# Four edits to a fused attention, MoE and soft-MoE kernel: zero products at the start, the remainder products moved, one copy moved to ScalarE, one weight load moved

## The chip, the core and the metric

The kernel runs on one core of a Trainium2 chip. The metric is the device time of one execution in microseconds, as the median of the executions timed.

## The reference, cut to what matters

Everything is float32. There are 4 batches, 12 heads, a sequence of S = 448 and a head size of 64.

```
scores = (q @ k.T) / 8 - log(448)
attn   = sigmoid(scores)              # no softmax: each score by itself
x      = (attn @ v), heads joined     # 1792 tokens x 768
x      = ((x @ w_a) * (x @ w_b)) @ w_out
logits = x @ phi                      # 32 columns
d      = softmax of logits over all 1792 tokens
c      = softmax of logits over the 32 columns
out    = c @ experts(d.T @ x)         # 8 experts, 4 slots each, two matrices w1, w2 with a relu between
```

## The kernel before

The heads are worked through in pairs: one step g of the attention is two heads, 6 steps to a batch, 24 in all (`NP` = 6, `GT0` = 13, `GQ` = 14). Of a step, `emit_TK` brings k and q into transposed form and splits each into a high and a low part (`split_heads`: a cast to fp32r and a subtraction), `emit_S` makes the scores of one chunk of keys as three products per head and hands each head's score tile to ScalarE (`sigmoid`, L249), and `emit_PV` multiplies with v. From step 13 on VectorE does the transposing (L191), before that TensorE (L195). From step 14 on a head's 448 keys are three chunks of 128 and a remainder of 64. The remainders of an even step and of the odd one after it share two tiles: `emit_S_rest` (L258) makes them, at the odd step's end, from `whole` (the q tile in place, and a copy of k's last 64 columns, `kr`, that ScalarE makes). `emit_PV` of the odd step ends with the products on them (L286).

`att()` is a generator that emits these pieces in a fixed order and yields after each. Nothing reorders them later: each engine runs its instructions in the order in which the program emits them. Around each piece the main loop (L1192) emits one step of whatever else is due: `fill_step` (the logits of a finished batch, `LG`, `logits`, `tokens`), `operands` (sums and splits of x for the products of batches 1 and 2, which go by a Strassen-like scheme in `unit`) and `prep_u` (the weights of the first unit, loaded by `load_u`).

PSUM has eight banks, shared out by tag: `ms` 2, `sc` 4, `ab` 2. `ms()` gives out the `ms` tag (later in the kernel, by a counter, also `sc`). A new tile of a tag takes a bank whose earlier tile has had its last reader, and the first instruction that writes it waits for that reader. Before the change the first chunk of step 13 (one head of two) and of the odd steps from 15 on is in `ms`, that of the even steps in `sc`; the remainders are in `ms`; `emit_PV` of steps 12 and 13 is in `ms`, from 14 on in `ab`; the logits of batch 0 are in `ab`, and the tile into which `tokens` transposes them (L935) is in `ms`. VectorE reads that tile out (L936).

The stages in time: batch 0's attention to 54 us, its two MoE products with batch 1's attention to 205, the attention of batches 2 and 3 to 280, the products of batches 1 and 2 (`unit`, L855) to 440, those of batch 3 (L667) to 544, and then the experts, whose weights come through a ring of SBUF slots that earlier stages leave free.

All loads of q, k and v are issued by SP in program order (`load_qkv`). The load for step g + 3 is emitted in `emit_TK` of step g, but for the q of steps 19 and 23, which `emit_S_rest` of steps 15 and 19 emits.

Of the kernel before, what the change touches and what calls it, by code (L numbers as in the profile page):

```python
# [41 lines left out]
def body(ctx, tc, q, k, v, w_a, w_b, w_out, phi, w1, w2, out):  # L42
# [68 lines left out]

    def consts():
        make_identity(nc, ident)
        dve.memset(nlog, -math.log(S))
        dve.memset(tiny, 2.0 ** -120)
        act.activation(rs, nlog, AF.Sigmoid)
        dve.tensor_tensor(e32, idj[:, 0], idj[:, 1], op=ALU.add)
        dve.tensor_tensor(e32, e32, idj[:, 2], op=ALU.add)
        dve.tensor_tensor(e32, e32, idj[:, 3], op=ALU.add)
        for j in range(1, 4):  # L120
            dve.tensor_copy(selF[:, j], e32)
# [8 lines left out]
    def load_qkv(g, names):  # L130
# [6 lines left out]
        for src, nm, n in ((k, "k", 3), (q, "q", 3), (v, "v", 3)):  # L137
# [31 lines left out]
            if nm == "v":  # L169
                t = t[:T].rearrange("p (h c d) -> p h c d", h=2, c=C)  # L170
                sp.dma_start(out=t, in_=s)
            else:
                t = t[:T].rearrange("p (c h d) -> p c h d", c=C, h=2)
                for h in range(2):
                    (sp if g or not h else act).dma_start(out=t[:, :, h], in_=s[:, h])
# [11 lines left out]
    def transposed(g, nm):  # L187
        a = qkv_t.pop((nm, g))
        if g >= GT0:
            a = a.rearrange("p n d -> p (n d)")  # L190
            dve.transpose(a, a)  # L191
            return a
        t = ms()
        for c in range(C):
            pe.transpose(t[:, c * T:(c + 1) * T], a[:, c].rearrange("p h d -> p (h d)"), ident[:T, :T])  # L195
        load_qkv(g + 3, nm)
        run["trans"] = True
        return t

    def emit_TK(g):  # L200
        if g >= B * NP:
            return
        if g >= GT0:
            for nm in "kq":
                t = transposed(g, nm)
                split_heads(g, nm, t, dve.tensor_copy)
                if g >= GQ:
                    if nm == "k":
                        kr = atp.tile([128, 64], F32, tag="kr", name="kr", bufs=3)
# [7 lines left out]
        if not g:  # L217
            tq = transposed(g, "q")
# [11 lines left out]
    def emit_S(g, chunks):  # L230
# [3 lines left out]
        for c in chunks:  # L234
            ab = (g < NP or 2 * NP < g < GQ) and c == 2
            by_ms = c == 0 and (g % 2 if g >= GQ else g >= GT0)
# [15 lines left out]
    def emit_S_rest(g):  # L252

        sc = [ms() for _ in range(2)]
# [65 lines left out]
    def att():  # L320
# [3 lines left out]
        for g in range(B * NP + 1):  # L324
# [8 lines left out]
            for c in first:  # L333
                emit_S(g, (c,))
                run["done"] = True
                yield 800
            if g:
# [22 lines left out]
            else:  # L360
# [7 lines left out]
                if g >= GQ and g % 2:  # L368
                    emit_S_rest(g)
                    yield 800  # L370
# [396 lines left out]
    def operands():  # L767
# [7 lines left out]
        for i in range(3):  # L775
            while 2 * NP + 3 + i not in xt:
                yield
# [107 lines left out]
    def logits(b):  # L885
# [11 lines left out]
        dve.tensor_reduce(mx, lf, axis=AX.X, op=ALU.max)  # L897
# [15 lines left out]
        if not b:  # L913
            dve.tensor_copy(ls, lf)
# [274 lines left out]
    then = [(GQ + 1, lambda: load_u(0)), (GQ + 5, lambda: reload_gk(0, 1, gk_01[1])),  # L1189
            (GQ + 6, lambda: load_u(1)), (GQ + 7, lambda: reload_gk(0, 0, gk_01[0])),  # L1190
            (GQ + 7, lambda: reload_gk(0, 2, gk_2))]
    for cost in att_g:  # L1192
# [5 lines left out]
        if next(ops, 0) == 0:  # L1198
# [226 lines left out]
```

## Time and profile before

| | us |
|---|---|
| median of 3 runs | 659.08 (658.64 to 660.87) |
| the profiled execution, its own time | 657.77 |
| span of the profiled execution, first to last instruction | 656.0 |

The profile is of one execution. Busy time of an engine is the sum over its instructions. PE is TensorE's products, PEld its weight loads, DVE is VectorE, ACT ScalarE, POOL GpSimd, SP the engine that issues most DMAs. A row of the timeline gives start and length in us, then engine, line, operation, and what is written from what; "x4" joins four such instructions, and brackets at the end give the engine's idle time before it and what ended that. A product in float32 stands as two instructions, one in fp32r as one.

### The profile page before, as it was taken

The page shows a single profiled execution, that of the slowest core. Times are in us where ns is not written, and L with a number is a line of the kernel's source. Part 1 is how long each engine was busy: PE and PEld are TensorE (multiplying, and loading weights), DVE is VectorE, ACT ScalarE, POOL GpSimd, SP SyncE. Part 2 cuts the span into 40 slices and gives each one's busy share as a digit, 9 for nine tenths or more (in the row PEclk, how much of TensorE's full clock was granted, in tenths as well). Part 3 has the DMA queues.
Part 4 walks back from the last instruction along what each step waited for, and adds up shares of the span by engine and source line. Part 5 has one row for each costly group of instructions (what it writes and reads, how often), then busy time and mean ns, then how long its engine had stood idle before and what let it go on. Part 6 is the DMA issues. An engine that isn't in the chain of part 4 may idle for free.

```text
span 656.0 us, 10813 instructions
## 1 busy us (share of the span) xinstructions
PE 626.3 (95%) x3967; PEld 445.3 (68%) x3967; DVE 382.2 (58%) x563; ACT 295.3 (45%) x532; POOL 308.7 (47%) x235
## 2 busy tenths in 40 slices
PE   6999999999999999999999999999999999996685
PEld 4457777777676555489988989887889885441121
DVE  4765788888773878688777776856243323030013
ACT  4888889889774677754423232201100002110012
POOL 0234687777644247569986576553335441000000
PEclk9999999999999999999999999999999999998897
DMA  9998999989968667911314333299899989999998
GB/s 212 273 263 236 298 305 285 310 280 297 286 162 190 133 132 157 252 36 48 97 49 104 99 103 82 72 252 306 242 379 407 419 284 389 415 402 415 409 363 295
DMA packets 149235, 159.74 MB, mean 244 GB/s; under 512 B 74480, under 2 KB 127312, under 8 KB 145104
## 3 DMA queue, kind: packets, MB, share of 16 engines
q1 hardware_dynamic: 146320, 157.35, 77.3%
q10 hardware_dynamic: 2864, 1.72, 0.9%
q8 instruction: 31, 0.51, 0.3%
q14 instruction: 20, 0.16, 0.1%
HBM read 129.11 MB, written 29.93 MB: 242 GB/s over the span
## 4 chain that ended last, share of the span: by engine, by line
PE 79%; DMA 14%; DVE 2%; ACT 2%; issue 1%; ACTq 1%; POOL 0%; SPq 0%; DVEq 0%; POOLq 0%
PE ab L667 26%; PE sc L855 16%; PE sc L243 8%; PE ab L855 8%; PE sc L273 5%; PE ab L279 3%; DMA misc<-clog 3%; DMA hp<-in_moe_w 2%; DMA e<-in_moe_w 2%; DMA eb<-in_moe_w 2%; PE ms L195 2%; PE ms L581 1%; DMA ea<-in_moe_w 1%; PE ms L956 1%; DMA lgp<-in_moe_w 1%; PE ms L479 1%
## 5 line engine op out<-in xcount | busy, mean ns | idle before, releaser
L453 POOL TENSOR_TENSOR w<-gk,cy 128x768 int32<-128x768 int32 x36 | 66.4, 1846 | 78.3 <-DVE gk L448 32.9
L249 ACT ACTIVATE a<-sc,sums 112x448 f32<-112x448 f32 (+1 forms) x147 | 83.0, 651 | 13.6 <-PE sc L243 13.5
L667 PE MATMUL ab<-t,wh 128*128 128x448 f32 x288 | 64.7, 371 | 0.3 <-DVE wh L550 0.3
L667 PEld LDWEIGHTS ab<-t,wh 128*128 128x128 f32 x288 | 53.6, 188 | 7.0 <-issue 1.3
L674 ACT COPY misc<-ab 128x448 f32<-128x448 f32 x24 | 12.7, 531 | 100.7 <-PE ab L667 100.7
L551 POOL TENSOR_TENSOR wl<-w,wh 128x768 fp32r<-128x768 f32 x24 | 45.7, 1908 | 9.7 <-ACT wh L550 9.6
L551 POOL TENSOR_TENSOR wl<-hp,wh 128x768 fp32r<-128x768 f32 x16 | 29.4, 1838 | 40.1 <-DVE wh L550 21.9
L273 PE MATMUL sc<-a,vn 112*64 112x448 f32 x192 | 38.7, 545 | 0.2 <-ACT a L249 0.2
L677 DVE TENSOR_TENSOR misc<-misc,ab 128x448 f32<-128x448 f32 x24 | 14.8, 615 | 39.2 <-PE ab L667 39.2
L243 PE MATMUL sc<-qh,kh 64*112 64x448 f32 (+1 forms) x147 | 34.8, 442 | 1.0 <-ACT qh L183 0.6
L667 PE MATMUL ab<-xh,wh 128*128 128x448 f32 x144 | 34.9, 377 | 0.0
L667 PE MATMUL ab<-xl,wh 128*128 128x448 f32 x144 | 34.8, 377 | 0.0
L1384 DVE COPY o<-sc 128x384 f32<-128x384 f32 x10 | 5.4, 554 | 49.9 <-PE sc L1362 48.8
L667 PE MATMUL ab<-xh,wl 128*128 128x448 f32 x144 | 34.3, 374 | 0.0
L667 PE MATMUL ab<-t,wl 128*128 128x448 f32 x144 | 34.3, 373 | 0.0
L735 ACT CAST wx<-T 128x384 fp32r<-128x384 f32 x19 | 9.7, 512 | 53.9 <-DVE T L757 35.9
L736 POOL TENSOR_TENSOR wx<-hp,wx 128x384 fp32r<-128x384 f32 x27 | 31.5, 1173 | 2.1 <-ACT wx L735 2.1
L446 DVE TENSOR_SCALAR mf<-gk 128x768 f32<-128x768 f32 x24 | 22.7, 946 | 16.6 <-ACT gk L429 16.6
L667 PEld LDWEIGHTS ab<-xl,wh 128*128 128x128 f32 x144 | 25.9, 188 | 9.5 <-issue 7.7
L243 PEld LDWEIGHTS sc<-qh,kh 64*112 64x112 f32 (+1 forms) x147 | 16.4, 200 | 21.2 <-issue 12.5
L667 PEld LDWEIGHTS ab<-xh,wh 128*128 128x128 f32 x144 | 25.7, 188 | 6.6 <-issue 4.3
L667 PEld LDWEIGHTS ab<-t,wl 128*128 128x128 f32 x144 | 26.6, 188 | 5.1 <-issue 2.0
(499 smaller groups left out, 1576.8 us busy)
## 6 DMA issues: line engine op xcount, KB each, us to landing
hp<-ab SPq DMA_DIRECT2D x14, 768.0 KB, 4.4
gk<-gk SPq DMA_DIRECT2D x44, 224.0 KB, 4.4
ab<-w SPq DMA_DIRECT2D x24, 384.0 KB, 7.5
eb<-in_moe_w SPq DMA_DIRECT2D x7, 1024.0 KB, 14.4
ea<-in_moe_w SPq DMA_DIRECT2D x7, 1024.0 KB, 11.5
eb<-in_moe_w SPq DMA_DIRECT2D x7, 768.0 KB, 15.0
ea<-in_moe_w SPq DMA_DIRECT2D x7, 768.0 KB, 15.1
wr_cv<-in_moe_w_a SPq DMA_DIRECT2D x6, 768.0 KB, 7.8
```

Of the source, the lines that this page charges most:

```text
L195: pe.transpose(t[:, c * T:(c + 1) * T], a[:, c].rearrange("p h d -> p (h d)"), ident[:T, :T])
L243: pe.matmul(sc[h], kx[r, cs], qx[r], start=(i == 0), stop=(i == 2))
L249: act.activation(a, sc, AF.Sigmoid, bias=nlog[:n], scale=1.0 / math.sqrt(D))
L273: pe.matmul(pv[64 * h:64 * h + 64], qkv_t["v", g][:, h, c, :], a_t.pop((g, h, c)), start=(c == 0), stop=(c == C - 1))
L279: pe.matmul(pv[64 * h:64 * h + 64], qkv_t["v", g][:, h, c], a_t.pop((g, h, c)), start=(c == 0), stop=False)
L446: dve.tensor_scalar(mf, m, LOW, HIGH, op0=ALU.max, op1=ALU.min)
L453: pool.tensor_tensor(thirds(w), m.bitcast(I32), thirds(cy_t.pop(x)), op=ALU.add)
L551: pool.tensor_tensor(wl, t, wh.bitcast(F32), op=ALU.subtract)
L667: pe.matmul(t, w[:, kk * 128:(kk + 1) * 128], xt[b * NP + kk][xi], start=(s == 0 and kk == 0), stop=(s == 2 and kk == KD - 1))
L677: dve.tensor_tensor(g, g, t, op=ALU.mult)
L736: pool.tensor_tensor(w[:, 1], t, w[:, 0].bitcast(F32), op=ALU.subtract)
L855: pe.matmul(t, w[:, wi, k * 128:(k + 1) * 128], xs[ORDER[m], k][xi], start=(s == 0 and k == 0), stop=(s == 2 and k == 2))
```

## The change

- `spin(n)` issues n products of a 128x128 block of zeros with itself into an `ms` tile that nothing reads. VectorE first clears that block; six are issued before the first k, two between k's and q's transposing in step 0.
- The first k is loaded with the heads outermost in SBUF, one DMA per head as before, so that a row's four vectors of a head are in one piece; its transposing becomes eight products with the identity.
- From step 14 on the first chunk of every step is in `ms`. The remainders are in `sc`, and are emitted at the next even step, behind its first chunk (for steps 22 and 23, at the end). `kr` gets a fourth buffer.
- ScalarE copies the first logits from PSUM to SBUF, and VectorE takes their maximum from the copy. VectorE's own copy, which came after the maximum, goes.
- `load_u(0)` is emitted before the main loop, no longer once step 15 is done. `operands` yields 1 where it waits for x, and the main loop then lets `prep_u(0)` go a step on, once step 15 is done.

```diff
--- before.py
+++ after.py
@@ -109,7 +109,15 @@
     run["col"] = 0
     nlog, rs, tiny = sums[:, 16:17], sums[:, 17:18], sums[:, 18:19]
 
+    def spin(n):
+
+        t = ms((128, 128))
+        for _ in range(n):
+            pe.matmul(t, wa[:, :128], wa[:, :128], start=True, stop=True)
+
     def consts():
+        dve.memset(wa[:, :128], 0.0)
+        spin(6)
         make_identity(nc, ident)
         dve.memset(nlog, -math.log(S))
         dve.memset(tiny, 2.0 ** -120)
@@ -169,6 +177,10 @@
             if nm == "v":
                 t = t[:T].rearrange("p (h c d) -> p h c d", h=2, c=C)
                 sp.dma_start(out=t, in_=s)
+            elif nm == "k" and not g:
+                t = t[:T].rearrange("p (h c d) -> p h c d", h=2, c=C)
+                for h in range(2):
+                    (act if h else sp).dma_start(out=t[:, h], in_=s[:, h])
             else:
                 t = t[:T].rearrange("p (c h d) -> p c h d", c=C, h=2)
                 for h in range(2):
@@ -192,6 +204,10 @@
             return a
         t = ms()
         for c in range(C):
+            if nm == "k" and not g:
+                for h in range(2):
+                    pe.matmul(t[64 * h:64 * h + 64, c * T:(c + 1) * T], a[:, h, c], ident[:T, :T], start=True, stop=True)
+                continue
             pe.transpose(t[:, c * T:(c + 1) * T], a[:, c].rearrange("p h d -> p (h d)"), ident[:T, :T])
         load_qkv(g + 3, nm)
         run["trans"] = True
@@ -206,7 +222,7 @@
                 split_heads(g, nm, t, dve.tensor_copy)
                 if g >= GQ:
                     if nm == "k":
-                        kr = atp.tile([128, 64], F32, tag="kr", name="kr", bufs=3)
+                        kr = atp.tile([128, 64], F32, tag="kr", name="kr", bufs=4)
                         act.copy(kr, t[:, 384:])
                         t = kr
                     whole[nm, g] = t
@@ -215,6 +231,7 @@
             return
         tk = transposed(g, "k")
         if not g:
+            spin(2)
             tq = transposed(g, "q")
         split_heads(g, "k", tk, dve.tensor_copy)
         if not g:
@@ -233,7 +250,7 @@
         n, _ = chunks_of(g)
         for c in chunks:
             ab = (g < NP or 2 * NP < g < GQ) and c == 2
-            by_ms = c == 0 and (g % 2 if g >= GQ else g >= GT0)
+            by_ms = c == 0 and g >= GT0
             sc = [ms((n, S)) if by_ms and (g >= GQ or not h) else ps_tile("ab" if ab else "sc", [n, S], 2 if ab else 4)
                   for h in range(2)]
             cs = slice(c * n, (c + 1) * n) if g < GQ else slice(c, 384, 3)
@@ -251,7 +268,7 @@
 
     def emit_S_rest(g):
 
-        sc = [ms() for _ in range(2)]
+        sc = [ps_tile("sc", [128, S], 4) for _ in range(2)]
         for d in range(2):
             for h in range(2):
                 r, f = slice(64 * h, 64 * h + 64), 64 * d
@@ -333,6 +350,9 @@
             for c in first:
                 emit_S(g, (c,))
                 run["done"] = True
+                yield 800
+            if g > GQ and g % 2 == 0:
+                emit_S_rest(g - 1)
                 yield 800
             if g:
                 if g < NP and more:
@@ -365,9 +385,6 @@
                     if c not in first:
                         emit_S(g, (c,))
                         yield 800
-                if g >= GQ and g % 2:
-                    emit_S_rest(g)
-                    yield 800
 
     PAIR = 860 + 4 * 800 + 3200
     att_g = att()
@@ -774,7 +791,7 @@
             yield
         for i in range(3):
             while 2 * NP + 3 + i not in xt:
-                yield
+                yield 1
             yield
             a11, a12, a21, a22 = (xt[n + i] for n in (NP, NP + 3, 2 * NP, 2 * NP + 3))
             s2 = cp.tile([128, S], F32, tag="s2", name="s2", bufs=2)
@@ -894,7 +911,9 @@
         if b:
             yield
         mx = col()
-        dve.tensor_reduce(mx, lf, axis=AX.X, op=ALU.max)
+        if not b:
+            act.copy(run["lsd"][0], lf)
+        dve.tensor_reduce(mx, lf if b else run["lsd"][0], axis=AX.X, op=ALU.max)
         nm = col()
         if b:
             dve.tensor_scalar(nm, mx, run["m"], -1.0, op0=ALU.max, op1=ALU.mult)
@@ -911,7 +930,6 @@
         turn = (lambda a, x: a.rearrange(x, t=32)) if b in TURNED else lambda a, x: a
         dt = turn(d, "p (t n) -> p n t")
         if not b:
-            dve.tensor_copy(ls, lf)
             run["exp"] = lambda: act.activation(dt, turn(ls, "p (n t) -> p n t"), AF.Exp, bias=nm, accum_out=sm)
             run["s"] = sm
             return
@@ -1186,7 +1204,8 @@
     pools["cp"] = cp_ctx.enter_context(tc.tile_pool(name="cp", bufs=1, side="left"))
     run["lsd2"] = (hps_t[0][:, 1536:1536 + S], hps_t[1][:, 1536:1536 + S], hps_t[2][:, 4 * S:4 * S + 128], hps_t[2][:, 4 * S + 128:])
     ops, pu = operands(), None
-    then = [(GQ + 1, lambda: load_u(0)), (GQ + 5, lambda: reload_gk(0, 1, gk_01[1])),
+    load_u(0)
+    then = [(GQ + 5, lambda: reload_gk(0, 1, gk_01[1])),
             (GQ + 6, lambda: load_u(1)), (GQ + 7, lambda: reload_gk(0, 0, gk_01[0])),
             (GQ + 7, lambda: reload_gk(0, 2, gk_2))]
     for cost in att_g:
@@ -1195,7 +1214,7 @@
         if not run.pop("trans", False):
             fill_step()
         run.pop("done", None)
-        if next(ops, 0) == 0:
+        if next(ops, 0) in ((0, 1) if GQ + 1 in xt else (0,)):
             pu = pu or prep_u(0)
             next(pu, None)
         if (4 * NP - 1, 0, C - 1) in a_t:
```

## Rows read from the trace of the kernel before

**Rows 1.** The chain that ended last: share of the span by engine.

```profile
PE 79%; DMA 14%; DVE 2%; ACT 2%; issue 1%; ACTq 1%; POOL 0%; SPq 0%; DVEq 0%; POOLq 0%
```

**Rows 2.** PE's waits, 200 to 560 us: total, times, longest (us).

```profile
PE ab L243 <- DVE hp L914: 1.3, 1, 1.3
PE sc L243 <- DVE ql L184: 0.5, 1, 0.5
```

**Rows 3.** The chain in order of time, 0 to 60: start us, us, what.

```profile
1.49 4.07 DMA qn<-in_q
...
5.61 1.02 PE ms L195 x4
...
7.24 2.58 PE sc L243 x12
9.82 1.33 PE ms L195 x8
...
12.56 0.54 PE ms L195 x4
```

**Rows 4.** Timeline of PE, 3 to 20 us: start, length, instruction.

```profile
3.98 0.98 PE L195 MATMUL ms<-ident,kn 112*128 112x112 f32 x4 [3.98 <-DMA kn<-in_k]
```

**Rows 5.** DMA packets moved from 0 to 4 us.

```profile
DMA packets 1597, 0.40 MB, mean 99 GB/s; under 512 B 1597, under 2 KB 1597, under 8 KB 1597
```

**Rows 6.** Timeline of all engines, 204 to 240 us.

```profile
214.58 0.62 DVE L897 TENSOR_REDUCE sums<-ab 128x1 f32<-128x448 f32 x1
...
215.30 0.61 DVE L914 COPY hp<-ab 128x448 f32<-128x448 f32 x1
...
215.97 0.46 PE L243 MATMUL ab<-qh,kh 64*112 64x448 f32 x1 [1.29 <-DVE hp L914]
...
217.37 0.40 PE L935 MATMUL ms<-ident,hp 32*112 32x32 f32 x4
...
217.70 0.54 PE L243 MATMUL sc<-qh,kh 64*128 64x448 f32 x2
...
218.57 3.23 PE L273 MATMUL ms<-a,vn 112*64 112x448 f32 x16
...
221.96 0.62 DVE L184 TENSOR_TENSOR ql<-qn,qh 128x448 fp32r<-128x448 f32 x1
...
222.50 0.28 DVE L936 COPY hp<-ms 112x128 f32<-112x128 f32 x1
```

**Rows 7.** Timeline of PE, 220 to 282 us.

```profile
226.24 0.54 PE L243 MATMUL sc<-qh,kh 64*128 64x448 f32 x2
...
227.73 0.98 PE L258 MATMUL ms<-qn,kr 64*64 64x448 f32 x8
228.65 0.54 PE L243 MATMUL sc<-qh,kh 64*128 64x448 f32 x2
...
229.53 2.48 PE L279 MATMUL ab<-a,vn 128*64 128x448 f32 x12
```

**Rows 8.** Timeline of ScalarE, 204 to 282 us.

```profile
227.28 2.21 ACT L249 ACTIVATE a<-sc,sums 128x448 f32<-128x448 f32 x4 [1.11 <-PE sc L243]
...
230.53 1.21 ACT L249 ACTIVATE a<-sc,sums 128x448 f32<-128x448 f32 x2
```

**Rows 9.** Timeline of SP's DMA issues, 198 to 285 us.

```profile
235.85 2.10 SPq L153 DMA_DIRECT2D qn<-in_q  x4
...
240.29 2.04 SPq L153 DMA_DIRECT2D gk<-in_q  x4
...
243.55 0.59 SPq L718 DMA_DIRECT2D hp<-ab  x1
```

**Rows 10.** Timeline of VectorE, 204 to 290 us.

```profile
241.51 0.63 DVE L191 STREAM_TRANSPOSE qn<-qn 128x448 f32<-128x448 f32 x1
...
279.86 0.62 DVE L308 COPY hp<-ab 128x448 f32<-128x448 f32 x1 [7.19 <-PE ab L286]
```

**Rows 11.** One window: PE, PEld, DVE, ACT, POOL, granted clock, DMA.

```profile
622.00:624.00 2.00, 1.40 (x10) 0.28 (x12) 0.00 (x0) 0.00 (x0) 0.00 (x0) 0.50 1.07 375
```

## The prediction

> **What bounds the kernel now.** I read the chain that ended last first: 79% of it is TensorE and 14% DMA [rows 1]. Laid out in time, the DMA share is its first five microseconds and the experts' weights after 550 us. Those come through slots that earlier products free, at fixed places in the program, so I take a shift of the front as a shift of the end, one for one. Next I read what TensorE waited for between 200 and 560 us, for a gain in the front has to be a wait or a cost there. There are two waits that this change can reach: 1.3 us for VectorE's copy of the first logits and 0.5 us for a low part of q [rows 2]. Third, the first 13 us in order of time: k lands at 3.98, is transposed, q lands at 5.56 (1.49 + 4.07), is transposed in 1.02, ScalarE casts it, and the first twelve score products take 2.58 [rows 3, 4]. Twelve such products later take 1.49 (226.24 to 227.73) [rows 7], and four transposes 0.54 in place of 1.02 [rows 3]: TensorE runs at about half its pace up to some 10 us. So the front has three prices: the late q, the slow products, and 1.8 us of waits.
>
> **The start.** Of what the slow pace costs, 1.1 is in the score products (2.58 less 1.49), 0.4 in q's transposing (1.02 less 0.6) and 0.3 in the next step's (1.33 for eight against twice 0.54): 1.8 in all. The pace rose behind the first score products, which ran without a gap; the transposes before them, with gaps between, did not bring it up. Twelve float32 instructions of 448 columns, two side by side, take 2.48 [rows 7], so one alone takes 0.41, one of 128 columns 0.12, and 0.24 at the slow pace. The six zero products are twelve of these, 2.8 us from about 1 us on, when VectorE has cleared their block; then come k's products and two more zero products, so TensorE has work almost without a gap until q lands. If the pace is up by then, all of the 1.8 is saved. If it rises no sooner, nothing is, and TensorE may get to q late: k's sixteen instructions of 112 columns, two side by side, take 1.65 at the slow pace and the two zero products 0.95, from 3.6 to 6.2 against a landing at 5.3, 0.9 late. As for the k load, its packets are of 256 bytes (0.40 MB in 1597 [rows 5]), and q, as large, lands 1.6 behind k; a quarter as many packets for k bring q forward by something from 0 to 0.5, and I take 0.3. Together I take a gain of 1.4, nearer to the full one because the gaps are filled, with bounds of 2.3 and - 0.6.
>
> On the k load the Trainium skill, "DMA: Bandwidth & Descriptors", section "Why small descriptors are slow (HBM only)", says that each packet carries a fixed overhead that weighs at 256 bytes. By that the 0.3 would be 0.5 and the forecast 0.2 lower; no row here has the same load in pieces of 1 KB.
>
> **The first logits.** VectorE gets to their maximum and copy only at 214.58 to 215.91 [rows 6]. ScalarE's copy stands behind step 13's first sigmoids in its own line and frees the `ab` bank sooner. TensorE's wait of 1.29 at 215.97 shrinks by something from 0 to 1.29, and I take all of it; VectorE's line gets the copy's 0.61 shorter.
>
> **Step 14's first chunk is where I see a new wait.** It moves from `sc` to `ms`, with both heads. It comes right behind the transposing of the logits (L935 at 217.37, chunk at 217.70), and that transposing's result holds one of the two `ms` banks until VectorE has copied it out. VectorE does so at 222.50 to 222.78, because that copy stands behind all of step 15's transposing and splitting, whose last instruction is at 221.96 [rows 6]. Before, the chunk took `sc` banks and didn't care. After, TensorE reaches it at about 216.4 (217.70 less 1.29), issues the first head's first product, and the second head's waits for VectorE: 222.78 less the 0.61 of the copy that is gone, 222.2. The chunk (0.88, from 228.65 to 229.53 [rows 7]) ends near 223.0. Behind it is step 13's product with v, in `ms` too: it needs the bank that the first head's sigmoid frees, one sigmoid of 0.55 (2.21 for four [rows 8]) and its start-up later, 223.7. It began at 218.57 [rows 6]. So TensorE is 5.2 later there, whether or not the wait of 1.29 is gone before it. Queued behind are all later products; nothing on VectorE or SP hangs on them at once, so nothing there pays it back. The lower bound, if the bank is free in time, is under the rivals.
>
> TensorE then stands idle for some 5.5 us. The granted clock reads 0.50 in a window behind broken work near the end [rows 11], which is the 1.2 GHz level, and at the start the slow pace cost 1.6 in the score products and transposes that followed. So the products behind the wait may run slow for a while: 0 to 1.6; I take 0.9.
>
> **The remainders.** A run of score products costs 0.27 beyond its products: twelve take 1.49, six 0.88 [rows 7], so six cost 0.61. With the remainders behind the next first chunk, that chunk joins the run before it and saves 0.27, at four steps (16, 18, 20, 22): 1.1. Against it: the remainders now need the `sc` banks that the second of four sigmoids frees, at about 227.28 + 1.1 = 228.4 against a start at 228.34, up to 0.1; and their sigmoids come last in ScalarE's line and end where the first chunk's do now, 231.74 [rows 8], against the products on them that would start near 231.7, up to 0.1. So 0.3 to 1.1 less; I take 0.5. A rest of this edit is on SP: the q of step 19 is loaded where the remainders are emitted, and now stands behind the k and q of step 20. It would be issued where the q of step 20 is now (240.29 to 242.33) and not at 235.85 [rows 9], while VectorE takes it at 241.51 [rows 10]. With TensorE some 4 later, that hides it; without, see the rivals.
>
> **The first unit's weights.** The load's 0.59 on SP [rows 9] moves ahead of the k and q of step 17, whose use is many steps off; SP has the same work up to 243.55, so the later loads don't move: 0, at most 0.6 where a load is short of time. VectorE's casts and GpSimd's sums move forward by up to two steps. VectorE has 7.19 idle ahead of 279.86 [rows 10], so TensorE gains nothing from weights that are ready sooner. What it gains is that GpSimd no longer works beside the split of step 22's q: the 0.5 wait goes [rows 2]. If that work instead delays another split, TensorE, being late, covers it: 0.
>
> **The sum.** Against the profiled execution's own time of 657.77 (span 656.0, 1.8 around it): + 5.2 + 0.9 - 1.4 - 0.5 - 0.5 = + 3.7, so 661.5. The median of the runs shown is 659.08, 1.3 more; the same 3.7 on it gives **662.8**, 0.56% slower. With all bounds the case runs from + 1.3 (no slow clock, 2.3 at the start, 1.1 from the remainders) to + 7.1 (1.6 for the clock, 0.6 lost at the start, 0.3 from the remainders, the wait for q not gone), so 660.4 to 666.2.
>
> **The rivals.** *The banks are free* (the other side): the copy out of the transposed logits isn't where VectorE's row at 222.50 puts it, or is overtaken, and neither the chunk nor the product with v waits. For it speaks only that TensorE waits at none of these places now; against it the row itself, and that VectorE never idles between 214 and 222. Then 1.29 + 1.4 + 0.5 + 0.5 are gained: 655.4. It decides from the point where the copy out ends before 216.4.
>
> *Only the short wait*: the logits' bank is free, but the product with v waits for the sigmoid: it starts near 217.9, 0.6 earlier than now. Then TensorE comes early to step 19, whose q is issued until 242.33 + 0.6 and lands later still, while it is taken at 241.51 now. That is at least 1.4 late and takes back the 0.6 and half of the remainders' gain: what stays is the start and 0.3, 1.7 in all, 657.4.
>
> *The clock falls for long behind the wait.* The window at 0.50 [rows 11] speaks for it; it would bring 1.6 in place of 0.9: 663.5, inside the first case's range. The Trainium skill, "TensorE: Matmul & The Clock Gate", section "HAM oscillation — how this bites in real kernels", describes just this: a wait that is long enough puts the clock back to half and the next work pays for it. By that the wait of 5.5 costs the full 1.6.
>
> **How the numbers follow.** The long wait gets 0.70 (the long clock penalty 0.25 of it): the code's order and the row at 222.50 both have to mislead me for it to fail. The short wait gets 0.17, free banks 0.13. A measurement here can tell about 0.3%, 2.0 us. Of the 0.70, 0.62 is slower by more and 0.08 within; of the 0.17, 0.11 is within and 0.06 faster; of the 0.13, 0.12 faster and 0.01 within. That is faster 0.18, same 0.20, slower 0.62. The range of the likeliest case is 660.4 to 666.2. To leave out no more than 2 in 10 it has to reach over the short wait to the nearer part of the free banks, and may stop short of the far end of the bounds: 656.6 to 666.0.
>
> **What would show it.** Right: in the profile after, a wait of TensorE of some 5 us at L243, tile `ms`, released by VectorE's L936, and step 13's product with v some 5 later against the first score product than now (211.3 between 7.24 and 218.57). The score products at the start at 0.2 apart and not 0.37 show the zero products' part; the copy's L914 gone with no wait on `ab` the third; first chunk and run before it without a 0.27 between them the fourth. Wrong: no idle time of TensorE above 1 us between 216 and 224 (minus the shift of the start), or a wait for step 19's q above 2 us, or a start that loses time because q's transposing waits behind k's products and the zero products.

## The result, and the profile after

The changed kernel takes 669.51 us (median of five runs, 667.68 to 672.05), the kernel before 659.08 in the same job: ratio 1.0146, interval 1.0111 to 1.0181, so 9.6 us slower by the ratio, 7.3 to 11.9. The forecast was 662.8, with a range to 666.0: slower, as said, and by the wait that was said, but 2.6 times as much. The profiled execution, the longest of the five, took 672.05 (span 670.3).

What TensorE waited for in the first 300 us (line waited for, us in total, times, longest):

```profile
PE ms L260 <- DVE hp L954: 6.2, 1, 6.2
PE ms L260 <- ACT a L266: 1.3, 1, 1.3
PE ms L116 <- DVE sums L123: 1.1, 1, 1.1
PE ms L496 <- POOL w L470: 0.9, 1, 0.9
PE ab L684 <- POOL wl L568: 0.9, 1, 0.9
PE sc L260 <- ACT qh L195: 0.6, 1, 0.6
```

The 1.3 for VectorE's copy of the first logits and the 0.5 for a low part of q [rows 2] are gone; 6.2 and another 1.3 (at step 22's first chunk) are new. The place itself, TensorE's instructions in order of time (start, us, engine, line, operation, idle time before and releaser; they answer to [rows 6, 7]):

```profile
217.40 0.40 PE L953 MATMUL ms<-ident,hp 32*112 32x32 f32 x4
217.73 0.53 PE L260 MATMUL ms<-qh,kh 64*128 64x448 f32 x1
224.47 0.74 PE L260 MATMUL ms<-qh,kh 64*128 64x448 f32 x1 [6.21 <-DVE hp L954]
...
226.38 5.73 PE L290 MATMUL ms<-a,vn 112*64 112x448 f32 x16 [0.42 <-ACT a L266]
232.04 0.54 PE L260 MATMUL sc<-qh,kh 64*128 64x448 f32 x2
```

And VectorE's:

```profile
223.59 0.62 DVE L196 TENSOR_TENSOR ql<-qn,qh 128x448 fp32r<-128x448 f32 x1
224.14 0.28 DVE L954 COPY hp<-ms 112x128 f32<-112x128 f32 x1
```

The first head's product of step 14's first chunk is issued at 217.73, the second head's stands until VectorE, behind all of step 15's splitting, has copied the transposed logits out; then the product with v waits for one sigmoid. It starts at 226.38, in before at 218.57. And it takes 5.73 where it took 3.2. The granted clock of that stretch (window, its length, busy time of PE with its instructions in brackets, PEclk, DMA share, GB/s):

```profile
215.00:220.00 5.00, 3.26 (x27) 1.00 0.76 195
220.00:225.00 5.00, 0.53 (x2) 0.62 1.01 164
225.00:230.00 5.00, 4.58 (x15) 0.50 0.85 190
230.00:235.00 5.00, 5.00 (x32) 0.85 0.53 82
```

In the wait the clock goes from its 2.4 to its 1.2 GHz level (0.50) and stays there through nearly all of the product with v, which ends at 232.1.

To place all of the loss I compare products one by one. The offset is the start of a TensorE product in one profile less the start of the same product in the profile of before; the table has the median over a stretch (given in before's time). A row is the profile of one execution.

```
offset, us                      150-188  206-214  223-226  276-300  560-580
changed                           -0.68    +1.77   +10.32   +12.73   +14.38
changed, profiled again           +2.14    +2.23   +10.93   +13.36   +15.24
changed, old place of the sums    -1.05    -1.05    +8.04    +9.04   +10.21
changed, wait filled              -1.67    -1.67    +4.04    +6.49    +6.74
changed, ScalarE copies out       -0.37    -0.37    +4.62    +7.08    +8.25
changed, chunk in sc              -1.13    -1.12    -1.32    +4.77    +5.39
  the same, order of loads        -1.38    +0.17    -0.04    +2.66    +4.53
before, chunk in ms               +0.48    +0.48    +8.97    +8.96   +10.11
before, start                     -0.65    -0.65    -0.63    -0.64    +0.79
before, ScalarE copies            +0.20    +0.20     0.00    +0.26    +0.57
before, weights sooner            +0.59    +0.59    +0.61    +2.23    +2.88
before, remainders                +0.95    +0.95    +0.97    +3.58    +4.16
  the same, last pair in place    +0.95    +0.95    +0.96    +1.37    +2.49
all waits out                     -0.80    -0.80    -1.72    -0.68    +0.74
  the same, weights sooner        -1.23    -1.23    -2.14    +0.44    +0.97
```

So in the changed kernel 8.55 are lost at step 14 (10.32 less 1.77), and 2.41 at steps 20 to 22 (12.73 less 10.32). The 2.4 between 188 and 206 in its first profile isn't the change's: profiled again it lost 0.1 there (last experiment).

### The profile page after: what moved, and what is told of

The parts are those of the page before. It is cut to its first block, busy times and chain, and to the rows that moved or that the text cites. A ratio compares the mean times of both kernels' runs of the same rounds, so it can differ in the third digit from the quotient of the medians.

```text
span 670.3 us, 10857 instructions
## 1 busy us (share of the span) xinstructions
PE 633.6 (95%) x3995; PEld 449.7 (67%) x3995; DVE 380.0 (57%) x563; ACT 296.1 (44%) x533; POOL 309.8 (46%) x235
## 3 DMA queue, kind: packets, MB, share of 16 engines
q10 hardware_dynamic: 2528, 1.72, 0.8%
## 4 chain that ended last, share of the span: by engine, by line
PE 77%; DMA 13%; POOL 2%; ACT 2%; DVE 2%; SPq 1%; issue 1%; ACTq 0%; DVEq 0%; POOLq 0%
PE ab L684 25%; PE sc L872 16%; PE ab L872 7%; PE sc L260 6%; PE sc L290 5%; DMA misc<-clog 3%; DMA e<-in_moe_w 2%; DMA eb<-in_moe_w 2%; DMA hp<-in_moe_w 2%; PE ab L296 2%; DMA ea<-in_moe_w 1%; PE ms L211 1%; PE ms L598 1%; DMA hp<-ab 1%; PE ms L290 1%; PE ms L496 1%
## 5 line engine op out<-in xcount | busy, mean ns | idle before, releaser
L260 PE MATMUL sc<-qh,kh 64*112 64x448 f32 (+1 forms) x137 | 31.5, 429 | 1.0 <-ACT qh L195 0.6
L753 POOL TENSOR_TENSOR wx<-T,wx 128x384 fp32r<-128x384 f32 x21 | 22.4, 1065 | 14.5 <-ACT wx L752 14.5
```

The lines of the kernel that those rows point to most:

```text
L260: pe.matmul(sc[h], kx[r, cs], qx[r], start=(i == 0), stop=(i == 2))
L753: pool.tensor_tensor(w[:, 1], t, w[:, 0].bitcast(F32), op=ALU.subtract)
```

## Experiments

Each was timed beside the kernel before on the same chip (before's medians there: 657.9 to 658.6).

**1. Step 14's first chunk in `ms`, alone in the kernel before; and back in `sc`, alone in the changed kernel.**

```diff
-            by_ms = c == 0 and (g % 2 if g >= GQ else g >= GT0)
+            by_ms = c == 0 and (g % 2 or g == GQ if g >= GQ else g >= GT0)
```

> The kernel before with that one edit alone: step 14's first chunk in ms. Theory: TensorE reaches the chunk at 217.7, VectorE's copy out ends at 222.8, the product with v starts near 224.4 and not at 218.6, and the products behind it run slow for about 2.5: 8.3 more than before, 667.4 (666 to 669). Rival 1 (the wait is made up later, since TensorE waits elsewhere anyway): 659 to 662. Rival 2 (the wait counts, the clock does not): 664.9.

```diff
-            by_ms = c == 0 and g >= GT0
+            by_ms = c == 0 and g >= GT0 and g != GQ
```

> The changed kernel with step 14's first chunk back in sc, all else as changed. Theory (most of the loss is TensorE's wait for the ms bank that the transposed logits hold, 6.2, a little for the sigmoid behind it, 0.4, and the slow clock after it, about 2.5): the wait at L260 for VectorE's L954 is gone, step 13's product with v starts within 1 us of the kernel before and takes 3.2 and not 5.7, and the time falls by about 8.5 to 661 (659.5 to 663). Rival 1 (most of the loss is the first unit's weights): less than 3 off, 667 or more. Rival 2 (the wait only goes to another place, step 19's q that is now issued late): the product with v starts early, but a wait of 1.5 to 3 stands at steps 18 to 19, 663 to 665.

Alone it takes 667.24, ratio 1.0138 (1.0121 to 1.0154), 9.1 more: the expected 667.4. This one edit is as large as the whole loss. The other way round, 663.12, ratio 1.008 (1.0062 to 1.0098): half of the loss stays, as rival 2 had it. The wait for `hp` shrinks to 1.2 (at step 15's first chunk, in `ms` before too), and TensorE, now in time, runs into step 19's q:

```profile
246.95 0.54 PE L260 MATMUL ms<-qh,kh 64*128 64x448 f32 x2 [2.71 <-DVE qh L195]
...
248.43 0.74 PE L260 MATMUL ms<-ql,kh 64*128 64x448 f32 x2 [0.59 <-DVE ql L196]
249.10 4.75 PE L296 MATMUL ab<-a,vn 128*64 128x448 f32 x12
```

SP's queue in the same run:

```profile
237.64 3.81 SPq L161 DMA_DIRECT2D gk<-in_q  x4
241.55 1.99 SPq L161 DMA_DIRECT2D qn<-in_q  x4
```

SP issues step 19's q (`qn`) at 241.55, behind step 20's k and q (`gk`), as the prediction had it (240.29 to 242.33). And again the product with v, 2.48 otherwise, takes 4.75 behind the wait.

**2. The loads in the order q of step 19, k and q of step 20** (in the run with the chunk in `sc`).

```diff
-                if nm == "k" or g not in (GQ + 2, GQ + 6):
+                if g != GQ + 3 and (nm == "k" or g not in (GQ + 2, GQ + 6)):
                     load_qkv(g + 3, nm)
...
             load_qkv(g + 4, "q")
+            load_qkv(g + 5, "kq")
```

> The changed kernel with step 14's first chunk in sc and, besides, the loads for the steps behind put in the order: q of step 19, then k and q of step 20 (in the run with the chunk in sc, SP issued step 19's q last, it landed at 245.6 and TensorE waited 2.7 + 0.6 and then ran its products with v at 4.7 and not 2.4). Theory: the q is issued some 2.4 sooner, that wait is 0.3 or less, the slow products behind it are gone, and the time falls from 663.1 by 5 to 658 (657 to 659.5). Rival 1 (the q's load is bound by its buffer, which the remainders free, not by SP's order): 1.5 or more of the wait stays and the clock with it, 661 or more. Rival 2 (k of step 20 is now late): the wait moves one step on, 660 to 662.

660.58, ratio 1.0029 (1.0015 to 1.0044): 3.4 less by the ratios, not 5. The q is issued at 238.47, VectorE waits 2.1 for it and not 5.4, TensorE no longer waits at step 19, and the slow product is gone. Two waits for VectorE's split of q remain, at other steps: 0.6 at step 20, as VectorE's line is still late by that 2.1, and 1.0 at step 22, where the changed kernel waits 1.3. So the order of SP was all of the wait at step 19 but not all of what is lost behind it.

**3. ScalarE copies the transposed logits out** (chunk still in `ms`): `act.copy` for `dve.tensor_copy` in `tokens` for the first batch.

> The changed kernel (chunk still in ms) with ScalarE, not VectorE, copying the transposed logits out of their ms bank. Theory (what holds the bank is VectorE's line, so another engine frees it): TensorE's wait of 6.2 becomes 1 or less, the product with v takes 3.2, and TensorE, now early, waits at step 19 for its late q (2.7 + 0.6, and 2.3 for the slow products behind it, as in the run with the chunk in sc): 663.5 (662 to 665) where before is 658.4 and the changed kernel 668.0. Rival (the bank is held by something else, such as the sigmoids): 667 or more.

664.92, ratio 1.0106 (1.0085 to 1.0126). The time lies at the upper end of what was expected, but by luck: the wait is 3.2, not 1, the product with v is still slow, and step 19's q isn't waited for. ScalarE in order of time:

```profile
218.87 0.24 ACT L226 COPY kr<-kn 128x64 f32<-128x64 f32 x1 [1.46 <-DVE kn L203]
219.02 0.26 ACT L954 COPY hp<-ms 112x128 f32<-112x128 f32 x1
```

TensorE behind it:

```profile
219.33 0.74 PE L260 MATMUL ms<-qh,kh 64*128 64x448 f32 x1 [3.20 <-ACT hp L954]
...
221.26 5.15 PE L290 MATMUL ms<-a,vn 112*64 112x448 f32 x16 [0.44 <-ACT a L266]
```

ScalarE's copy stands behind its copy `kr`, and that waits for VectorE's transposing of step 15's k: the bank is still held by VectorE's line, by way of another engine. A wait half as long costs three quarters as much in the product behind it (5.15 and 5.73, against 3.23 at full clock).

**4. The price of the clock: products of the identity in the wait** (nothing reads them).

```diff
+        if g == GQ and 0 in chunks:
+            t = ps_tile("sc", [128, 128], 4)
+            for _ in range(26):
+                pe.matmul(t, ident, ident, start=True, stop=True)
```

The diff is that of 26 products; the first try had 40, from which 665.3 was expected. They took 9.2, more than the wait itself; the product with v then took 3.23, and the time was 668.05. With 20:

> As the run with 40 products of the identity in the wait, which took 9.2 and not 5 (each is two instructions) and so more than the wait; now 20 of them, 4.6. Theory: the first chunk goes on when VectorE is done, as without them; the granted clock stays at 1.00, the product with v takes 3.2 and not 5.7, and the time falls by 2.4 from 668.0 to 665.6 (664.6 to 666.6). Rival (the slow products have another cause): 668.0 or more.

668.24, ratio 1.015 (1.012 to 1.0179): missed, and the time is the rival's. But the profile doesn't bear the rival out: the 20 left a wait of 1.56 and one of 0.59, the clock read 0.50 behind them, and the product with v still took 4.92. With 26:

> The changed kernel with 26 products of the identity ahead of step 14's first chunk: 6.1 us by the 4.73 of 20, as long as the wait (20 left 1.6 of it and the product with v still took 4.9; 40 were too long, and it took 3.2). Theory (the clock falls in any wait of about two microseconds, for much the same price): the idle time left is below 0.5, the chunk goes on when VectorE is done, the product with v takes 3.2 to 3.4 and not 5.7, and the offset behind it is 2.5 to 3 less than without the products: 665 where the changed kernel is 667.6. Rival (only the work that is in the way counts, the clock is no cost): 667.6.

TensorE in order of time:

```profile
214.30 6.07 PE L254 MATMUL sc<-ident 128*128 128x128 f32 x52
...
221.07 0.54 PE L264 MATMUL ms<-qh,kh 64*128 64x448 f32 x1 [0.24 <-DVE hp L958]
...
222.60 3.23 PE L294 MATMUL ms<-a,vn 112*64 112x448 f32 x16 [0.59 <-ACT a L270]
```

Its windows, columns as above:

```profile
220.00:225.00 5.00, 4.17 (x24) 1.00 0.82 190
225.00:230.00 5.00, 5.00 (x36) 1.00 0.71 123
```

665.52, ratio 1.0103 (1.0074 to 1.0131). VectorE frees the bank as late as ever, the clock stays at 1.00, and step 14 costs 5.71 (4.04 and 1.67) where it costs 8.55 and 8.70 in the two profiles of the changed kernel: the slow clock alone is 2.9, the wait 5.7. By the times the 2.9 is less sharp: 1.0103 against 1.0146, whose intervals overlap, and against 1.0165 for the changed kernel beside it on the same chip (experiment 9), whose interval just doesn't.

**5. The first unit's weights**: the sums back in their place in the changed kernel; sooner in the kernel before (the diff of the change, alone); sooner in the version with all waits out (8).

> The changed kernel with GpSimd's first-unit weight sums back where they were (only the load stays early). Theory (the weights' sums stand in GpSimd's line ahead of the operands' sums that the splits of steps 18 to 20 and the first unit wait for, some 2.4): 667.1 (666 to 668). Rival 1 (my prediction's step: TensorE is late there and covers it): no change, 669.5, and the offset between the two kernels grows at 256 to 279 us all the same. Rival 2 (the early sums gain 0.5): 670.0.

> The kernel before with the first unit's weights sooner and nothing else (load first, GpSimd's sums two steps earlier). Theory: GpSimd's line is longer ahead of the operands' sums and TensorE waits 2 to 3 more around 256 to 280 us: 661.5 (660.5 to 662.5). Rival 1 (my prediction's term): 0.5 less, 658.6. Rival 2 (only together with the wait at step 14 does it cost): 659.1.

> The kernel with all the waits out (1.0016 times before, 659) with the first unit's sums sooner again, as the change has them. Theory (the sums on GpSimd and the casts on VectorE stand ahead of the splits of steps 18 to 20, whatever comes before): TensorE waits 1.5 to 2.5 more between 245 and 275, and the time is 660.5 to 661.5 where before is 658. Rival (my prediction's step, covered or a gain): 658.5 to 659.

The first gives 667.62, ratio 1.014 (1.0119 to 1.016), which can't be told from the changed kernel; the second 660.57, ratio 1.0036 (1.0023 to 1.0049), 2.4 more, inside what was expected; the third 660.22, ratio 1.0025 (1.0008 to 1.0042) against 1.0016 without, not told apart either. The offsets are sharper: between the columns 223-226 and 276-300 they grow by 2.41, 2.43, 2.45 and 2.46 in four profiles with the remainders moved and the sums sooner (the changed kernel's two, the wait filled, ScalarE copying out), and by 1.00 with the sums in the old place; without the wait at step 14 by 2.58 with them and 1.04 without; alone by 1.62. So the sums cost 1.4 to 1.6. How, in the run of before with them alone, VectorE in order of time:

```profile
259.13 0.39 DVE L763 CAST S2h<-s 128x448 fp32r<-128x448 f32 x1 [1.04 <-POOL s L783]
...
263.34 0.40 DVE L183 CAST qh<-qn 128x448 fp32r<-128x448 f32 x1
```

TensorE's waits there, in steps 21, 22 and 23:

```profile
258.14 0.54 PE L243 MATMUL ms<-ql,kh 64*128 64x448 f32 x2 [0.24 <-DMA qn<-in_q]
...
263.88 0.54 PE L243 MATMUL sc<-qh,kh 64*128 64x448 f32 x2 [0.39 <-ACT a L249]
...
270.69 0.54 PE L243 MATMUL ms<-qh,kh 64*128 64x448 f32 x2 [0.71 <-DVE qh L183]
```

GpSimd's sum `s`, in before and in that run:

```profile
254.63 1.30 POOL L783 TENSOR_TENSOR s<-misc,t 128x448 f32<-128x448 f32 x1
257.57 1.53 POOL L783 TENSOR_TENSOR s<-misc,t 128x448 f32<-128x448 f32 x1
```

The unit's sums stand ahead of it in GpSimd's line (243 to 248 us, in before at 260 to 265), so GpSimd gets to the operands' sum `s` 2.9 later, where TensorE is 0.6 late; VectorE's cast of it waits 1.04, and queued behind that cast are the splits of steps 22 and 23. The split of step 22's q does get quicker, as the prediction had it (0.63 in place of 1.31), but it starts 1.9 later, behind that cast. (The 0.24 is put down to a load of q; the 0.39 is put down to ScalarE, but VectorE's `qh` ends at 263.74, just ahead of it.)

**6. The remainders alone** in the kernel before, with a fourth buffer for q so that step 19's q is loaded with the others; and the same with the last pair in its old place:

```diff
-            if g > GQ and g % 2 == 0:
+            if g > GQ and g % 2 == 0 and g != GQ + 8:
                 emit_S_rest(g - 1)
...
+                if g == GQ + 7:
+                    emit_S_rest(g)
```

> The kernel before with the remainders behind the next first chunk, in sc, the first chunks from step 16 on in ms, and a fourth buffer for q so that step 19's q is not late; nothing else. My prediction's term: 0.5 less (0.3 to 1.1). Theory (the remainders' products take 1.15 to 1.32 and not 0.91, as their sc banks come free late, which eats the 0.27 that the joined run saves): 0, the offset between 225 and 262 within 0.3. Rival (the fourth buffer or the banks cost elsewhere): 1 or more later.

> The run with the remainders alone, but the remainders of steps 20 and 21 ahead of step 22's first chunk, as before; those of the three earlier pairs stay behind the next first chunk. Theory (behind it, the 0.9 of the remainders no longer cover VectorE's split of step 22's q: TensorE waits 0.7 + 0.5, the granted clock reads 0.50 behind it and the product with v takes 3.7 and not 2.5; that is all that the edit costs): the offset against the profile of before grows by 0.3 or less between 225 and 270, not by 2.6, and the time is 658.3 (657.3 to 659.3) where the other was 660.2 and before is 658.6. Rival (the fourth buffer for q or the banks of the earlier steps cost it): 1.5 or more is lost there all the same, 660.

Alone 660.19, ratio 1.0027 (1.0011 to 1.0043): 1.8 slower where the prediction had 0.5 gained and I, by then, nothing. Nearly all of it is at one place (TensorE in order of time):

```profile
262.96 0.54 PE L242 MATMUL ms<-qh,kh 64*128 64x448 f32 x2 [0.72 <-ACT a L248]
...
264.21 0.54 PE L242 MATMUL ms<-ql,kh 64*128 64x448 f32 x2 [0.51 <-DVE ql L184]
264.68 1.42 PE L257 MATMUL sc<-gk,kr 64*64 64x448 f32 x8
266.03 3.68 PE L276 MATMUL ab<-a,gk 128*64 128x448 f32 x12
```

VectorE at the same time, and the window behind:

```profile
262.28 0.53 DVE L183 CAST qh<-qn 128x448 fp32r<-128x448 f32 x1
262.84 1.32 DVE L184 TENSOR_TENSOR ql<-qn,qh 128x448 fp32r<-128x448 f32 x1
```

```profile
266.00:268.00 2.00, 2.00 (x10) 0.50 0.92 288
```

This is step 22's first chunk. In before the 0.9 of the remainders stood ahead of it and covered most of VectorE's split of its q (the wait of 0.5 [rows 2] is the rest). Moved behind it, they cover nothing: 0.72 and 0.51 of wait. In this profile the clock then falls to 0.50 and the product with v takes 3.68 and not 2.48, 1.2 of the 2.6 that the offset grows by. That part isn't the edit's each time. The changed kernel with the sums in their old place waits as long at the same place:

```profile
270.07 0.54 PE L260 MATMUL ms<-qh,kh 64*128 64x448 f32 x2 [0.77 <-ACT a L266]
...
271.33 0.53 PE L260 MATMUL ms<-ql,kh 64*128 64x448 f32 x2 [0.51 <-DVE ql L196]
...
272.70 2.48 PE L296 MATMUL ab<-a,gk 128*64 128x448 f32 x12
```

There, and in the version with all waits out (8), with 0.71 and 0.52, PEclk reads 1.00 throughout and the offset grows by 1.0. So the remainders cost 1.0 to 1.4 by the waits, and 1.2 more where the clock falls; what decides that it falls is open. With that pair back ahead of the chunk (and the fourth buffer kept), the waits are gone (TensorE, same stretch):

```profile
262.54 1.69 PE L257 MATMUL sc<-gk,kr 64*64 64x448 f32 x8 [0.17 <-ACT a L248]
264.15 0.54 PE L242 MATMUL ms<-qh,kh 64*128 64x448 f32 x2
...
265.03 2.48 PE L276 MATMUL ab<-a,gk 128*64 128x448 f32 x12
```

659.07, ratio 1.0004 (0.9984 to 1.0023); the offset grows by 0.4 there and not by 2.6. The three other pairs gain and lose nothing: what joining the runs saves, the remainders' products give back: from their start to the next product's it is 1.15 to 1.6, not 0.91. That they wait for `sc` banks is the likely reason; no run changes that alone.

**7. The start alone, and ScalarE's copy of the first logits alone.**

> The kernel before with the edit of the start alone (zero products, k in 1 KB pieces and by products, two more zero products ahead of q). My prediction's term: 1.4 less, 656.6 where before is 658.0. Theory now (the offsets of six profiles at 16 us: -0.7, -1.2, -1.3 with the edit, 0, +0.5, +0.6 without): 1.4 on the mean (1.0 to 1.8), of which the profile shows the score products at 1.7 and not 2.6, and q's transposing late by up to 1.0 behind the slow products. Rival: the products in the way eat the gain, 658.0.

> The kernel before with ScalarE copying the first logits, alone. My prediction's step: TensorE's wait of 1.29 goes and the time falls by 1.3, to 656.7 where before is 658.0. Theory now (seen in the run with step 14's chunk in sc): step 15's first chunk, in ms, then stands some 1.2 before VectorE's copy out of the transposed logits is done, so most of the 1.29 turns into that wait: 0.2 to 0.8 gained, 657.5. Rival: the copy delays step 13's sigmoids on ScalarE and costs as much: 658.0 or more.

The start: 658.33, ratio 0.9996 (0.9976 to 1.0016), no gain that can be told; the 1.4 forecast would be 0.9979, still inside the interval. Over the profiles, the first column (the table doesn't show all) is -0.75 on the mean of the 14 with the edit (-1.67 to +2.14) and +0.53 on that of the six without, before's own 0 among them (to +0.95): 1.3 gained. What spreads the first group is when the products become quick. Two of the same edit, the first with the wait filled, the second the changed kernel profiled again:

```profile
1.05 2.93 PE L116 MATMUL ms<-wa 128*128 128x128 f32 x12 [1.05 <-DVE sums L123]
3.91 0.99 PE L209 MATMUL ms<-ident,kn 112*64 112x112 f32 x16
...
5.60 0.60 PE L211 MATMUL ms<-ident,qn 112*128 112x112 f32 x4
```

```profile
1.05 2.93 PE L116 MATMUL ms<-wa 128*128 128x128 f32 x12 [1.05 <-DVE sums L123]
3.91 1.76 PE L209 MATMUL ms<-ident,kn 112*64 112x112 f32 x16
5.60 1.23 PE L116 MATMUL ms<-wa 128*128 128x128 f32 x4
6.88 1.01 PE L211 MATMUL ms<-ident,qn 112*128 112x112 f32 x4
```

The same zero products, in the same 2.93; then k's products take 0.99 or 1.76, and q's transposing starts at 5.60 or at 6.88, at the quick or the slow pace. By then q has long been there. SP and ScalarE's queue issue it at 1.19 and 1.20 and not at 1.50 and 1.49, as the issues of k ahead of it take 0.4 and not 0.7, and its later half lands 3.4 to 3.5 behind its issue, not 4.1: at some 4.6 to 4.7 in place of 5.56. So TensorE would not have had to wait for q, and the two zero products ahead of its transposing (0.71 to 1.23) stand in its way.

The copy: 658.12, ratio 0.9999 (0.998 to 1.0017), no gain that can be told; all of the 1.3 would be 0.998, the interval's end. The 1.29 goes, and 1.2 stands at step 15's first chunk, whose `ms` bank the transposed logits hold (the list of TensorE's waits):

```profile
PE ms L243 <- DVE hp L937: 1.2, 1, 1.2
```

**8. All waits out, and what of it pays.** The changed kernel with the chunk in `sc`, ScalarE copying the transposed logits out, the fourth buffer for q, the sums in the old place; besides, the same with the last pair of remainders in place, and the kernel before with the start, ScalarE's two copies and the buffer.

> The changed kernel with step 14's first chunk in sc, ScalarE copying the transposed logits out, a fourth buffer for q so that step 19's q is loaded with the others, and the first unit's sums where they were. Theory (the change loses by these waits alone): TensorE waits nowhere above 0.7 between 200 and 300, and what is left of the change gains 1.3 at the start, 1.2 at the first logits and 0.5 by the remainders: 655.4 (654.4 to 656.6) where before is 658.4. Rival (TensorE, early, only meets the next load or cast): a wait of 1 to 2 at steps 17 to 21, 657 to 659.

> The run with all the waits out (1.0016 times before), with the remainders of steps 20 and 21 as before as well. Theory: the 1.1 that it lost at 250 to 265 shrinks to 0.5 or less, and the time is 0.6 to 1 below that run's: 658 to 658.6 where before is 658.6, no gain that can be told. Rival (what was lost was the clock behind that wait alone, and all of it comes back): 657 or less, faster than before.

> The kernel before with the edit of the start, both copies of the first logits by ScalarE and a fourth buffer for q; the remainders, the even steps' first chunks and the weights as before. Theory: 1.3 and 1.2 less, 655.9 (654.9 to 657.1) where before is 658.4; the remainders' edit is worth the difference to the run that has it, 0.5 by my prediction, 0 by the changed kernel's profile, in which the remainders' products took 1.15 to 1.25 and not 0.91. Rival (the next load or cast takes it back): 657 to 659.

658.53, ratio 1.0016 (0.9997 to 1.0035); 658.49, 0.9996 (0.9978 to 1.0015); 657.32, 0.9996 (0.9975 to 1.0017). None can be told from the kernel before. The first and the third were expected 655.4 and 655.9, and their rivals' times came; the second came as expected. In the table "all waits out" is 1.72 ahead behind step 14, 0.68 at 276 to 300 (steps 20 to 22), and 0.74 behind at 560 to 580. The last loss is a wait for VectorE's cast of late w_a and w_b blocks (L567 in the changed kernel, 2.0 there, 0.3 in before); each profile of an edited kernel has between 0.25 and 2.6 of it, also those whose edits are far away. Why was not settled; there is one profile of the kernel before, and it may be that one that is low.

**9. The changed kernel again.**

> The changed kernel once more, beside the others on this chip. Theory: 667.6 where before is 658.0 (1.0146); the 2.4 that its first profile lost between 190 and 203 (GpSimd's split of the w_a and w_b blocks, a DMA before it) is not there, as in none of the other profiles; the wait at step 14 is 6.2, the slow products 2.5, and 256 to 280 costs 2.4. Rival: the 2.4 at 190 to 203 is part of the change, and is there again.

670.03, ratio 1.0165 (1.0135 to 1.0194), more than the 667.6 expected, but the interval overlaps that of the first time. The wait is 6.2 again, the product with v takes 5.88, step 14 costs 8.70, steps 20 to 22 2.43; the loss at 188 to 206 isn't there.

## Why the prediction was right in sign and too small

Three terms of the sum failed: the slow clock (+ 0.9 forecast, + 2.9 measured), the remainders (- 0.5, + 1.0) and the first unit's weights (- 0.5, + 1.4). The long wait, on which the sign rested, was right.

- **The wait at step 14** was right in place, holder, and what follows it, 5.2 forecast, 5.7 measured; the chunk's edit alone, with the slow clock behind it, costs 9.1. Most of the 0.5 is the copy that is gone from VectorE's line: that was to bring the copying of the transposed logits 0.61 forward, and brought 0.13 (224.14 less the offset of 1.77, against 222.50), as the cast behind it took 0.84 and not 0.38. The long wait is the case that the forecast rested on, and *the banks are free* and *only the short wait* fell with it.
- **The slow clock** is the term that was mis-sized: 0.9, bounds 0 to 1.6; it measured 2.9. I took its price from the start, from what the slow pace had cost the score products and transposes there [rows 3, 4]. The price is that of the work that stands behind the wait: here one long product with v, 5.73 in place of 3.2, and the chunk ahead of it. No bound reached that far. The rival *the clock falls for long* was the right one, with the same wrong price. The Trainium skill, "TensorE: Matmul & The Clock Gate", section "HAM oscillation — how this bites in real kernels", says that the next work after such a wait starts at half clock: the trace agrees (0.50 at 225 to 230), and the 2.9 is this case's own figure.
- **The remainders** failed in sign: - 0.5 forecast; in the offsets + 1.0 in company, + 2.6 alone (1.2 of it a slow clock that came in one of three profiles with these waits), 0.4 without the last pair. The step counted what joined runs save and looked for the cost in the remainders' own banks and sigmoids, where it just cancels. It did not ask what the remainders had covered: step 22's q, whose wait of 0.5 stood in [rows 2].
- **The first unit's weights** failed in sign: - 0.5, with "TensorE, being late, covers it: 0"; it costs 1.4 to 1.6. Being 10 late covers nothing here, since GpSimd's line is fed by the same steps and is late by as much: with the sums in their old place its two last `s` come 8.1 and 8.2 later than in before, where TensorE is 8.0 late, and with the sums sooner 14.4 and 12.8 later, where TensorE is 10.3 late. The premise that VectorE has 7.19 idle ahead of 279.86 [rows 10] was true and didn't help: the wait is some 20 us before that, inside VectorE's line, at a cast.
- **Step 19's q** is covered when TensorE is late, as said: no wait for it in the changed kernel; 2.7 and 0.6 with the chunk in `sc`.
- **The start**, 1.4 forecast, 1.3 in the offsets, with a spread as wide as the bounds. The landing of q came 0.9 forward and not 0.3, which paid nothing, since TensorE came to q after it had landed.
- **The first logits**: the wait of 1.29 goes, but alone it is worth nothing: step 15's first chunk then waits 1.2 for the transposed logits' bank. In the changed kernel the gain is lost in the long wait, as the forecast had it.

Measured: 5.7 + 2.9 - 1.3 + 1.0 + 1.4 = 9.7, against 9.6 by the ratio and 10.4 between the medians (669.51 and 659.08); the rest lies within what the casts before 560 vary. Of the 6.0 between that and the forecast 3.7, 2.0 are the clock, 1.5 the remainders, 1.9 the weights, 0.5 the wait, 0.1 the start.

*A shift of the front is a shift of the end* held for the large losses. For gains it is not shown: every version that is early behind step 14 (by 0.6 to 2.1) is late by 0.7 or more at 560 to 580, but the loss before 560 is in the late versions too, and the times can't tell a gain of 1.3.

## What to carry to other kernels

Moving a tile to another pair of buffers means asking who holds each of them at that moment and where the releasing instruction stands in its own engine's line. Of work that is moved, ask what it was covering, not only what it needs; here a wait of half a microsecond behind it in the profile was the sign that it covered something with nothing to spare. And price a stall with the slow work behind it: here 5.7 of wait brought 2.9 more, and a wait of 1.6 with 0.6 close behind it 1.7.

## What the runs showed of the hardware

- The price of the clock shrinks less than the wait does. The same product with v (3.23 at full clock) took 5.73, 5.88 and 6.24 behind a wait of 6.2 (the changed kernel twice, and with the sums in their old place), 5.57 behind 4.6 (the chunk alone in the kernel before), 5.15 behind 3.2, and 4.92 behind 1.56 and 0.59.
- Behind short waits the clock does not fall each time. Of three kernels with 0.7 to 0.8 and 0.5 close together at step 22's first chunk, one fell to 0.50 behind them and two stayed at 1.00. It stayed there too behind a single 1.3 at that place (the changed kernel) and a single 1.2 before step 15's chunk (the chunk in `sc`).
- Six zero products, twelve instructions without a gap from 1.05 on, do not fix when the pace rises: k's products behind them took 0.99 in one run and 1.76 in others, and in one the score products were slow up to 13 us. PEclk reads 1.00 in all of these first microseconds; there the pace can only be read from the durations.
